# A planned order of instructions made anew (later weight loads, ten early T buffers, three raw weight buffers), and the last output tile stored in two halves

## The chip, the cores and the metric

One NeuronCore of a Trainium2 chip runs the whole program. The metric is the device time of one execution in microseconds; lower is better. Three runs of the kernel before gave a median of 514.42 us (514.08 to 516.64).

## What is computed

Two stages follow each other. The first is a linear recurrence over 768 tokens for 4 batches of 8 heads of 48 dimensions; the second is a gated two-layer network on its 3,072 rows:

```python
# first stage, per batch and head
for t in range(S):                                   # S = 768
    cur = einsum('bhd,bhe->bhde', u * k[t], v[t])
    y[t] = einsum('bhd,bhde->bhe', r[t], state + cur)
    state = w * state + einsum('bhd,bhe->bhde', k[t], v[t])
# second stage, x = y as 3072 rows of 384
h = x @ w_in                                         # 384 x 2048
out = (h * cos(h)) @ w_out                           # 2048 x 384
```

The weights `w_in` and `w_out` arrive as 64-bit floats and are turned on the chip into a high and a low 32-bit part.

## The kernel before

**First stage.** The tokens are cut into 24 chunks of 128 tokens of one batch (`chunk`), in the order of time over all four batches. A chunk loads r, k and v (on the SP queue), multiplies r by k (POOL, L864), decays k (POOL, L874) and multiplies by u (POOL, L917), transposes k and r on TensorE (L833), forms a 128x128 product per head (L958), masks it (DVE, L963), multiplies by the state (L978) and by v (L989) into x, and makes the new state (L1004, DVE L1026 and L1027). x is split into a high and a low part (ACT L1179, DVE L1184). The first 12 chunks (`EARLY`) are done so, before and beside the start of the second stage; the other 12 are done later in halves of 64 tokens (`in_halves`, L1060 to L1123), between the matmuls of the second stage.

**Second stage.** Eight blocks of three chunks (384 tokens) go through 16 tiles of the hidden dimension, f = 0 to 15: 128 steps. A step has nine w_in matmuls (`mm_h`, L302), then a chain on ACT and DVE (L314, L317, L320, L1287, L1290, L1293), then nine w_out matmuls (`mm_o`, L309) into three PSUM accumulators. The first four blocks go through f = 0, 1, then through 2 to 4, then 5 to 9, then 10 to 15, and add their partial outputs in DRAM (`UNITS`, `CUTS`). So the first eight steps want only the tiles f = 0 and 1 of either weight.

**Weights.** `conv` turns one tile of raw weights into its two parts: a load on SP (w_in: six DMAs, L540; w_out: one, L561) into a buffer of the ring `R_raw`, ACT (L646), DVE (L654, L666), POOL (L677), ACT for the high part (L687), DVE for the low part (L694). There are 32 such tiles. `R_raw` has two buffers, and a third (`raw_r`) which is the memory of two of the four early r buffers (`r_all`) and comes free when the early chunks have used r. The ring `R_T`, from which a chunk takes four buffers, has eight.

**The order.** Every operation is an `Op` with an engine, a due date, a cost, a latency and the buffers that it takes. `Plan.order` makes the order of all engines before the program is built: `one_pass` picks, for each engine, among the operations that can start first the one with the earliest due date, and `latest` turns the result into new due dates for the next pass. The due dates of the first pass come from the program's formulas and from two tables of numbers, `CHUNK_DUE` and `TILE_SHIFT`. What comes out is one fixed order per engine; each engine, the SP queue too, works through its own list in that order and waits where an operand isn't there. Where the plan has TensorE idle before the first w_in matmul, `warm_up` puts matmuls on a zeroed tile (L1351), one for each 0.2 us of the planned gap.

**The end.** The last step's three w_out tiles of 384 columns are copied out of PSUM (ACT L1320, DVE L1322) and stored; the last one goes out on the ACT queue (L1331).

## Time and profile before

| what | value |
|---|---|
| median of 3 runs | 514.42 us (514.08 to 516.64) |
| profiled execution | 514.43 us, its span 512.7 us |
| TensorE busy | 498.7 us (97% of the span), 5,836 matmuls |
| DVE, ACT, POOL busy | 383.6, 314.0, 177.3 us |
| mean granted TensorE clock | 0.995 |
| data moved | 61.81 MB, 121 GB/s on the mean |

The span runs from the first instruction of the program to the last; the profiled execution's own time has 1.7 us around it. Times in the rows below are from the start of the span. A busy TensorE counts the warm-up matmuls too, so the first 60 us have to be read in the timeline. "Loads" are named here in units of 192 KB: r, k or v of one chunk is one unit, a raw weight tile of 384 KB two, and u one.

### The profile page before, as it was taken

The page shows a single profiled execution, that of the slowest core. Times are in us where ns is not written, and L with a number is a line of the kernel's source. Part 1 is how long each engine was busy: PE and PEld are TensorE (multiplying, and loading weights), DVE is VectorE, ACT ScalarE, POOL GpSimd, SP SyncE. Part 2 cuts the span into 40 slices and gives each one's busy share as a digit, 9 for nine tenths or more (in the row PEclk, how much of TensorE's full clock was granted, in tenths as well). Part 3 has the DMA queues.
Part 4 walks back from the last instruction along what each step waited for, and adds up shares of the span by engine and source line. Part 5 has one row for each costly group of instructions (what it writes and reads, how often), then busy time and mean ns, then how long its engine had stood idle before and what let it go on. Part 6 is the DMA issues. An engine that isn't in the chain of part 4 may idle for free.

```text
span 512.7 us, 14821 instructions
## 1 busy us (share of the span) xinstructions
PE 498.7 (97%) x5836; PEld 472.2 (92%) x5836; DVE 383.6 (75%) x788; ACT 314.0 (61%) x805; POOL 177.3 (35%) x183
## 2 busy tenths in 40 slices
PE   7999899999999999999999999999999999999994
PEld 5777789999999999999999999999999999999994
DVE  6888778889899996566777786767767777756452
ACT  1887676777776676547375665574663746654442
POOL 5876512246544463214426224133044042200000
PEclk9999899999999999999999999999999999999999
DMA  9978526577855875426484837448364475110001
GB/s 139 157 152 153 135 79 181 161 161 147 163 138 126 188 144 92 90 40 114 115 173 124 181 93 181 100 130 200 90 169 118 120 178 149 35 49 1 1 1 53
DMA packets 116657, 61.81 MB, mean 121 GB/s; under 512 B 80097, under 2 KB 112482, under 8 KB 116578
## 3 DMA queue, kind: packets, MB, share of 16 engines
q1 hardware_dynamic: 111250, 53.50, 43.0%
q0 software_dynamic: 5184, 7.08, 9.9%
q8 instruction: 47, 0.77, 0.7%
q14 instruction: 32, 0.26, 0.2%
q10 hardware_dynamic: 144, 0.20, 0.1%
HBM read 48.96 MB, written 11.80 MB: 118 GB/s over the span
## 4 chain that ended last, share of the span: by engine, by line
PE 88%; ACT 0%; issue 0%
PE psum L309 40%; PE psum L302 40%; PE psum L1123 4%; PE psum L1060 1%; PE psum L1076 1%; PE psum L989 1%; PE psum L958 0%; PE psum L978 0%; PE psum L1004 0%; PE psum L833 0%; ACT f L1320 0%; PE psum L605 0%
## 5 line engine op out<-in xcount | busy, mean ns | idle before, releaser
L309 PE MATMUL psum<-w_out_hi,gh 128*128 128x384 f32 x384 | 131.9, 344 | 0.0
L302 PE MATMUL psum<-xh,w_in_hi 128*128 128x384 f32 x384 | 131.5, 342 | 0.0
L309 PE MATMUL psum<-w_out_hi,gl 128*128 128x384 f32 x384 | 129.7, 338 | 0.0
L302 PE MATMUL psum<-xh,w_in_lo 128*128 128x384 f32 x384 | 129.7, 338 | 0.0
L309 PE MATMUL psum<-w_out_lo,gh 128*128 128x384 f32 x384 | 129.5, 337 | 0.0
L302 PE MATMUL psum<-xl,w_in_hi 128*128 128x384 f32 x384 | 129.4, 337 | 0.0
L314 ACT ACTIVATE qi<-psum 128x384 int32<-128x384 f32 (+1 forms) x132 | 62.9, 479 | 79.6 <-PE psum L302 78.8
L317 DVE SCALAR_TENSOR_TENSOR f<-psum,qi 128x384 f32<-128x384 f32 (+1 forms) x132 | 71.0, 540 | 47.4 <-ACT qi L314 46.6
L1293 DVE TENSOR_TENSOR gl<-f,gh 128x384 fp32r<-128x384 f32 (+1 forms) x132 | 83.9, 639 | 28.9 <-ACT gh L1290 28.0
L1290 ACT CAST gh<-f 128x384 fp32r<-128x384 f32 (+1 forms) x132 | 65.8, 501 | 40.0 <-DVE f L1287 20.0
L320 ACT ACTIVATE f<-f 128x384 f32<-128x384 f32 (+1 forms) x132 | 67.6, 514 | 30.9 <-DVE f L317 30.4
L1287 DVE TENSOR_TENSOR f<-psum,f 128x384 f32<-128x384 f32 (+1 forms) x132 | 70.6, 537 | 12.8 <-ACT f L320 10.9
L309 PEld LDWEIGHTS psum<-w_out_hi,gh 128*128 128x128 f32 x384 | 72.0, 187 | 2.4 <-issue 0.2
L302 PEld LDWEIGHTS psum<-xh,w_in_hi 128*128 128x128 f32 x384 | 72.5, 189 | 1.6 <-ACT T L942 0.2
L302 PEld LDWEIGHTS psum<-xl,w_in_hi 128*128 128x128 f32 x384 | 72.6, 189 | 0.0
L302 PEld LDWEIGHTS psum<-xh,w_in_lo 128*128 128x128 f32 x384 | 72.6, 189 | 0.0
L309 PEld LDWEIGHTS psum<-w_out_hi,gl 128*128 128x128 f32 x384 | 72.0, 188 | 0.0
L309 PEld LDWEIGHTS psum<-w_out_lo,gh 128*128 128x128 f32 x384 | 72.0, 187 | 0.0
L852 POOL TENSOR_TENSOR T<-T,decT_k 112x512 f32<-112x512 f32 x12 | 17.0, 1414 | 126.7 <-DVE T L847 50.8
L1335 POOL DMA_DIRECT2D out_dram<-f x36 | 33.3, 1080 | 41.0 <-ACT f L1320 40.6
L677 POOL TENSOR_TENSOR f<-f,raw 128x384 int32<-128x384 int32 x23 | 26.2, 1138 | 48.0 <-ACT gh L1290 15.7
L942 ACT ACTIVATE T<-ident,a 128x128 f32<-128x128 f32 x96 | 30.2, 391 | 1.2 <-DVE a L923 1.2
(124 smaller groups left out, 610.8 us busy)
## 6 DMA issues: line engine op xcount, KB each, us to landing
raw<-in_moe_w_out_dram SPq DMA_DIRECT2D x23, 384.0 KB, 3.6
out_dram<-f POOLq DMA_DIRECT2D x36, 192.0 KB, 5.0
raw<-in_moe_w_in_dram SPq DMA_DIRECT2D x72, 64.0 KB, 2.4
out_dram<-f SPq DMA_DIRECT2D x23, 192.0 KB, 2.0
r_all<-in_r_dram SPq DMA_DIRECT2D x40, 96.0 KB, 2.3
raw<-in_moe_w_in_dram SPq DMA_DIRECT2D x10, 384.0 KB, 4.0
raw<-in_k_dram SPq DMA_DIRECT2D x39, 96.0 KB, 2.2
v<-in_v_dram SPq DMA_DIRECT2D x18, 192.0 KB, 4.4
```

Of the source, the lines that this page charges most:

```text
L302: nc.tensor.matmul(ph, a, b_, start=(i == 0), stop=(i == len(mm) - 1))
L309: nc.tensor.matmul(acc, a[:, ts], b_, start=(first and i == 0), stop=(last and i == 2))
L314: nc.scalar.activation(qi, ph, AF.Copy, scale=INV_2PI, bias=0.25)
L317: nc.vector.scalar_tensor_tensor(q, ph, INV_2PI, qi, op0=ALU.mult, op1=ALU.subtract)
L320: nc.scalar.activation(q, q, AF.Sin, scale=TWO_PI, bias=0.5 * math.pi)
L677: lambda: nc.gpsimd.tensor_tensor(ai(), ai(), cn(), op=ALU.add),
L942: nc.scalar.activation(A[j]()[:, p, :], ident, AF.Copy, scale=ab()[:, h : h + 1])
L1123: nc.tensor.matmul(xv()[G * g : G * g + G, kk, tokens(n)], lhsT, rhs, start=(kk // 2, g) not in opened, stop=True, skip_group_check=True,)
L1287: nc.vector.tensor_tensor(g()[:, cs], ph()[:, cs], q()[:, cs], op=ALU.mult)
L1290: nc.scalar.copy(gh()[:, cs], g()[:, cs])
L1293: nc.vector.tensor_tensor(gl()[:, cs], g()[:, cs], f32(gh())[:, cs], op=ALU.subtract)
L1335: nc.gpsimd.dma_start(dst, ob(), accum_op=ALU.add)
```

## The change

The tables `CHUNK_SHIFT` (24 entries, added to due dates from one formula) and `TILE_SHIFT` (32 entries) replace the two old ones, and there are seven passes for six. In the plan, an operation that issues DMAs gets a time for which its data move (`dma`), the moves are taken one after another, and an issue counts as startable at the earliest 3 us before the moves ahead of it end; costs of some operations are others. The r buffers of the early chunks are four of their own (before: two of their own and two in `r_all`), so `R_raw` has three buffers of its own from the start. Early chunks take T buffers from ten. The parts of w_out kept from the start are 8 tiles for 10. Warm-ups may stand up to the first w_out matmul. The last w_out tile is computed, copied and stored as two halves of 192 columns, the first through DVE and the SP queue, the second through ACT and its queue. The matmuls and other operations are the same but for that tile and the warm-ups (78 for 65).

```diff
-CHUNK_DUE = (-17.2, -100.0, -17.0, -16.6, -14.0, -12.8, -11.2, -10.1, -1.3, 1.2, 13.7, 37.7)
-TILE_SHIFT = (-9.7, 1.9, -82.4, -2.9, -12.4, 2.4, -14.7, 11.2, 1.4, 0.6, 6.8, 16.5)
-PASSES = 6
+CHUNK_SHIFT = (
+    -11.6, -28.5, -0.3, -1.6, 3.2, -4.4, 2.1, -0.2, -0.1, -1.5, 1.6, 0.7, -6.4, -53.9, -19.5, 1.4,
...
+PASSES = 7
+DMA_AHEAD, DMA_FIRST, DMA_LAST, DMA_LAND = 3.0, 1.3, 0.6, 1.95
...
-                        feas.append((max(free[eng], r[0], port if o.port else 0.0), o, r[1]))
+                        t = max(free[eng], r[0], port if o.port else 0.0, moved - DMA_AHEAD if o.dma else 0.0)
+                        feas.append((t, o, r[1]))
...
+            if o.dma:
+                moved = max(moved, t + DMA_FIRST) + o.dma
+                o.lat = max(moved + DMA_LAST - o.end, DMA_LAND)
...
-    F_1 = CUTS[-2]
+    F_1 = NF // 2
...
-        r_all = att.tile([P, 2, H, DP], F32, name="r_all")
-        R_r = [Tile(r_all[:, i]) for i in range(2)]
-        raw_r = Tile(r_all.rearrange("q i h d -> q (i h d)")[:, 0 : 2 * DM].bitcast(I32).rearrange("q (f w) -> q f w", w=2))
...
-        X_r = early_ring("r", 2, [P, H, DP])
+        X_r, X_T = early_ring("r", 4, [P, H, DP]), early_ring("T", 2, [P, NP, C])
...
-        R_raw = ring("raw", 2, [P, DM, 2], I32) + [raw_r]
+        R_raw = ring("raw", 3, [P, DM, 2], I32)
...
-                rb, kb, vb = Buf(R_r + X_r), Buf(R_k + X_k), Buf(R_v + X_v)
+                rb, kb, vb = Buf(X_r), Buf(R_k + X_k), Buf(R_v + X_v)
...
-            kT, rT = Buf(R_T), Buf(R_T)
+            R_Tc = R_T + X_T if i < EARLY else R_T
+            kT, rT = Buf(R_Tc), Buf(R_Tc)
...
-                due = CHUNK_DUE[i]
+                due = -1.5 * (EARLY - i) - 1.0
...
+            due += CHUNK_SHIFT[i]
...
-            if i < len(TILE_SHIFT):
-                due += TILE_SHIFT[i]
+            due += TILE_SHIFT[i]
...
+                jc = FIRST[n] + t
+                last = jc == NJ - 1 and f == f1 - 1
+                ends = [slice(0, DM // 2), slice(DM // 2, DM)] if last else [slice(0, DM)]
+                for e, cs in enumerate(ends):
...
+                        mm_o(acc(), gh(), gl(), f, t, f == f0, f == f1 - 1 and cs.stop == DM, cs)
...
+                    eng = DVE if t % 2 or (last and e == 0) else ACT
...
+                    q = ACT if last and eng == ACT else POOL if f0 and not last else SP
```

How the order moves, at three places. On the SP queue, the loads of the last early chunks (k and r in pairs of DMAs of four heads each, v in one) and of the first weights; before:

```order
L540 DMA raw1_128<-in_moe_w_in_dram 32x2x256 x4
L540 DMA raw1_128<-in_moe_w_in_dram 64x256 x2
L763 DMA early_k1_90<-in_k_dram 128x4x48 x2
L763 DMA early_r0_95<-in_r_dram 128x4x48 x2
L755 DMA v2_83<-in_v_dram 128x8x48
L763 DMA early_k2_91<-in_k_dram 128x4x48 x2
L763 DMA early_r1_96<-in_r_dram 128x4x48 x2
L755 DMA early_v0_92<-in_v_dram 128x8x48
L561 DMA raw0_127<-in_moe_w_out_dram 128x768
```

and now:

```order
L551 DMA raw0_130<-in_moe_w_in_dram 32x2x256 x4
L551 DMA raw0_130<-in_moe_w_in_dram 64x256 x2
L782 DMA early_r2_96<-in_r_dram 128x4x48 x2
L782 DMA early_k1_89<-in_k_dram 128x4x48 x2
L774 DMA v2_82<-in_v_dram 128x8x48
L551 DMA raw1_131<-in_moe_w_in_dram 32x2x256 x4
L551 DMA raw1_131<-in_moe_w_in_dram 64x256 x2
L782 DMA early_r3_97<-in_r_dram 128x4x48 x2
L782 DMA early_k2_90<-in_k_dram 128x4x48 x2
L774 DMA early_v0_91<-in_v_dram 128x8x48
L774 DMA early_v1_92<-in_v_dram 128x8x48
L572 DMA raw2_132<-in_moe_w_out_dram 128x768
```

The first w_in tile (raw0) stood behind 21 units of r, k and v and now stands behind 28. The second (raw1) stood before k and r of the eleventh chunk and now stands behind them and its v. In front of the last load of the twelfth chunk there were 38 units (u, twelve k, twelve r, nine v, two raw tiles of two each, its own counted), and there are 38 now.

On POOL, the products of the last early chunk, `f<-early_r,early_k`, and the sums that end the conversion of a raw tile, `f<-f,raw`; before:

```order
L864 TENSOR_TENSOR f7_120<-early_r1_96,early_k2_91 128x384
L677 TENSOR_TENSOR f4_117<-f4_117,raw1_128 128x384
L874 TENSOR_TENSOR early_k2_91<-early_k2_91,dec_k_133 128x2x4x48
L917 TENSOR_TENSOR f7_120<-f7_120,u_b_129 128x384
L677 TENSOR_TENSOR f8_121<-f8_121,raw0_127 128x384
```

and now:

```order
L883 TENSOR_TENSOR f5_121<-early_r3_97,early_k2_90 128x384
L696 TENSOR_TENSOR f4_120<-f4_120,raw0_130 128x384
L893 TENSOR_TENSOR early_k2_90<-early_k2_90,dec_k_137 128x2x4x48
L936 TENSOR_TENSOR f5_121<-f5_121,u_b_133 128x384
L696 TENSOR_TENSOR f7_123<-f7_123,raw1_131 128x384
```

The sum behind the twelfth chunk's first product was that of the second w_in tile; it is now that of the first, and the second's comes three operations later.

On ACT now, from the high part of the first w_in tile to that of the second (`raw2` holds w_out for f = 0, and `raw0` by then w_out for f = 1, loaded a second time):

```order
L706 CAST w_in_hi_66<-f4_120 128x3x128
L961 ACTIVATE early_T0_98<-ident_64,a1_84 128x128 x4
L961 ACTIVATE T2_102<-ident_64,a1_84 128x128 x2
L1198 CAST xh_114<-psum_76 128x384
L961 ACTIVATE T2_102<-ident_64,a1_84 128x128 x2
L665 ACTIVATE raw2_132<-raw2_132 128x384
L665 ACTIVATE raw0_130<-raw0_130 128x384
L326 ACTIVATE qi0_125<-psum_76 128x384
L706 CAST w_in_hi_66<-f7_123 128x3x128
```

Before, the two casts of w_in stood 19 rows apart with only the second tile's own L646 between them; now the first passes over two w_out tiles stand ahead of the second cast.

On TensorE the list up to the second step's w_in matmuls holds the same work but for one chunk's products with state and v (L978 and L989 before, L997 and L1008 now): ahead of them stand 12 chunks' transposes, 11 chunks' L958, 9 of L1004 and the first step's nine w_in matmuls in either program, with 5 and 9 chunks of L978 and L989 before, and 6 and 10 now. The first step's matmuls stood behind the ninth chunk's transposes; they now stand directly ahead of the twelfth's.

## Rows read from the trace of the kernel before

**Rows 1.** The page's busy time of TensorE (part 1: busy us, share of the span, instructions) and the granted clock in 40 slices of the span (part 2, tenths of full speed).

```profile
PE 498.7 (97%) x5836; PEld 472.2 (92%) x5836; DVE 383.6 (75%) x788; ACT 314.0 (61%) x805; POOL 177.3 (35%) x183
...
PEclk9999899999999999999999999999999999999999
```

**Rows 2.** The page's part 4, the chain of waits that ended last: shares of the span by engine.

```profile
PE 88%; ACT 0%; issue 0%
```

**Rows 3.** Busy time by stretch. Columns: the stretch in us, its length, then for PE, PEld, DVE, ACT and POOL the busy us and the instructions in it, the granted TensorE clock, the DMA engines' share and what they moved.

```profile
10.00:20.00 10.00, 8.02 (x142) 6.66 (x144) 9.04 (x18) 6.37 (x20) 8.37 (x9) 1.00 1.33 155
20.00:30.00 10.00, 9.92 (x241) 8.17 (x237) 8.36 (x17) 9.58 (x29) 8.89 (x10) 1.00 0.89 162
30.00:40.00 10.00, 9.22 (x268) 7.19 (x270) 9.15 (x19) 8.64 (x26) 5.96 (x7) 1.00 0.71 141
40.00:50.00 10.00, 9.02 (x225) 7.37 (x213) 7.78 (x17) 6.69 (x20) 6.37 (x7) 1.00 0.78 158
50.00:60.00 10.00, 7.98 (x152) 6.90 (x135) 8.36 (x18) 7.18 (x22) 6.72 (x6) 0.86 0.87 186
...
100.00:150.00 50.00, 50.00 (x288) 50.00 (x287) 46.45 (x89) 35.99 (x82) 25.17 (x25) 1.00 0.68 152
```

**Rows 4.** The same view with finer stretches.

```profile
58.00:60.00 2.00, 2.00 (x8) 2.00 (x7) 1.84 (x4) 1.62 (x6) 0.00 (x0) 0.50 0.46 137
```

**Rows 5.** The chain of waits in order of time, merged: start us, us, what.

```profile
93.17 1.56 PE psum L302 x9
```

**Rows 6.** Timeline of TensorE. Columns: start us, us from the first start to the last end, line, operation, tiles, how many; in brackets the idle time before and what ended it.

```profile
49.56 0.67 PE L978 MATMUL psum<-T,s 48*32 48x128 f32 x32
50.16 1.08 PE L989 MATMUL psum<-T,v 128*32 128x128 f32 x32
51.17 0.56 PE L1004 MATMUL psum<-v,k 128*48 128x48 f32 x16
...
53.43 1.16 PE L958 MATMUL psum<-T,T 48*128 48x128 f32 x16
56.14 0.44 PE L833 MATMUL psum<-ident,early_k 64*112 64x64 f32 x8 [1.55 <-POOL early_k L874]
...
56.64 1.42 PE L958 MATMUL psum<-T,T 48*128 48x128 f32 x16
57.98 0.69 PE L302 MATMUL psum<-xh,w_in_hi 128*128 128x384 f32 x1
...
60.71 0.34 PE L302 MATMUL psum<-xh,w_in_lo 128*128 128x384 f32 x1
```

**Rows 7.** Timeline of POOL, same columns.

```profile
48.63 1.02 POOL L864 TENSOR_TENSOR f<-early_r,early_k 128x384 f32<-128x384 f32 x1 [3.47 <-DMA early_r<-in_r_dram]
...
53.13 1.01 POOL L864 TENSOR_TENSOR f<-early_r,early_k 128x384 f32<-128x384 f32 x1 [0.65 <-DVE a L923]
54.10 1.02 POOL L677 TENSOR_TENSOR f<-f,raw 128x384 int32<-128x384 int32 x1
55.07 1.01 POOL L874 TENSOR_TENSOR early_k<-early_k,dec_k 128x384 f32<-128x384 f32 x1
```

**Rows 8.** Timeline of the SP queue (SPq: the time in which SP issues the loads of a row, its waits included).

```profile
39.91 3.42 SPq L540 DMA_DIRECT2D raw<-in_moe_w_in_dram  x6
43.45 1.63 SPq L763 DMA_DIRECT2D early_k<-in_k_dram  x2
...
48.02 1.01 SPq L763 DMA_DIRECT2D early_r<-in_r_dram  x2
...
49.67 1.86 SPq L561 DMA_DIRECT2D raw<-in_moe_w_out_dram  x1
```

**Rows 9.** DMA issues from 0 to 84 us: tiles, queue, how many, KB each, median us from issue to landing.

```profile
early_r<-in_r_dram SPq DMA_DIRECT2D x12, 96.0 KB, 4.1
...
raw<-in_moe_w_out_dram SPq DMA_DIRECT2D x3, 384.0 KB, 3.2
```

**Rows 10.** What the SP queue waited for from 0 to 70 us: line, releaser, us in total, times, longest.

```profile
SPq L763 <- PE psum L989: 1.2, 1, 1.2
SPq L763 <- POOL f L864: 0.7, 2, 0.4
SPq L763 <- PE psum L302: 0.7, 1, 0.7
```

**Rows 11.** Timeline of DVE, two steps of the conversion of the second w_in tile.

```profile
50.10 0.54 DVE L666 SCALAR_TENSOR_TENSOR f<-raw,f 128x384 int32<-128x384 int32 x1
...
55.69 0.81 DVE L694 TENSOR_TENSOR w_in_lo<-f,w_in_hi 128x384 fp32r<-128x384 f32 x1 [0.23 <-ACT w_in_hi L687]
```

**Rows 12.** Timeline of ACT, the step between them.

```profile
55.15 0.51 ACT L687 CAST w_in_hi<-f 128x384 fp32r<-128x384 f32 x1 [1.52 <-POOL f L677]
```

**Rows 13.** Timeline of the end of the run.

```profile
505.64 0.34 PE L309 MATMUL psum<-w_out_lo,gh 128*128 128x384 f32 x1
506.02 0.48 ACT L1320 COPY f<-psum 128x384 f32<-128x384 f32 x1 [0.58 <-PE psum L309]
506.53 0.38 ACTq L1331 DMA_DIRECT2D out_dram<-f  x1
```

**Rows 14.** DMA issues from 505 us to the end.

```profile
out_dram<-f ACTq DMA_DIRECT2D x1, 192.0 KB, 3.4
```

**Rows 15.** Timeline of TensorE at the start, the four transposes of the decay table.

```profile
11.57 0.66 PE L501 MATMUL psum<-ident,decT_k 128*128 128x128 f32 x4 [1.79 <-DVE decT_k L485]
```

More of the change, by code (lines that the diff above doesn't have):

```diff
@@ L86, in __init__, with op @@
         self.lines = {}
-    def op(self, eng, due, cost, emit, after=(), bufs=(), lat=0.2, line=None, port=False):
-        o = Op(eng, due, cost, lat, emit, after, bufs, self.lines.get(line) if line else None, port)
+    def op(self, eng, due, cost, emit, after=(), bufs=(), lat=0.2, line=None, port=False, dma=0.0, behind=None):
+        o = Op(eng, due, cost, lat, emit, after, bufs, self.lines.get(line) if line else behind, port, dma)
         if line:
@@ L191, in one_pass @@
                 cand.setdefault(o.eng, []).append(o)
-        done, port = [], 0.0
+        done, port, moved = [], 0.0, 0.0
         while len(done) < len(self.ops):
@@ L308, in mm_o @@
         for i, (a, b_) in enumerate(mm):
-            nc.tensor.matmul(acc, a[:, ts], b_, start=(first and i == 0), stop=(last and i == 2))
+            nc.tensor.matmul(acc[:, cs], a[:, ts], b_[:, cs], start=(first and i == 0), stop=(last and i == 2))
     def whole(qi, ph):
@@ L639, in cn @@
                 return raw()[:, :, 0]
-            o0 = op(SP, due - 3.5, 1.6 if part else 3.2, lambda: load_raw(i, raw, True), [behind], [raw], lat=3.4)
+            o0 = op(
+                SP,
+                due - 3.5,
+                0.5 if part else 4.2,
+                lambda: load_raw(i, raw, True),
+                [behind],
+                [raw],
+                dma=1.4 if part else 1.5,
+            )
             o2 = op(
@@ L782, in chunk @@
                 ks, rs = Buf(R_raw), Buf(R_raw)
[L784 removed]
+            rbs = [rb]
             def load_r():
@@ L934, in early @@
             def early():
-                A = [Buf(R_T) for _ in range(2)]
+                A = [Buf(R_Tc) for _ in range(2)]
                 Ap = [Buf(B_ONE) for _ in range(2)]
@@ L1313 @@
                     ob = Buf(R_f)
-                    jc = FIRST[n] + t
                     row = (jc % B) * S + (jc // B) * C
-                    dst = out[row : row + C, :]
-                    def cp(acc=acc[t], ob=ob, t=t):
-                        if t % 2 == 0:
-                            nc.scalar.copy(ob(), acc()[:, 0:DM])
-                        else:
-                            nc.vector.tensor_copy(ob(), acc()[:, 0:DM])
-                    oc = op(ACT if t % 2 == 0 else DVE, s + 2.3, 0.45, cp, [oo], [acc[t], ob])
@@ L1327, with cp @@
-                    last = jc == NJ - 1
-                    def st(ob=ob, dst=dst, f0=f0, last=last):
-                        if last:
-                            nc.scalar.dma_start(dst, ob())
-                        elif f0 == 0:
-                            nc.sync.dma_start(dst, ob())
+                    dst = out[row : row + C, cs]
+                    eng = DVE if t % 2 or (last and e == 0) else ACT
+                    def cp(acc=acc[t], ob=ob, eng=eng, cs=cs):
+                        if eng == ACT:
+                            nc.scalar.copy(ob()[:, cs], acc()[:, cs])
+                        else:
+                            nc.vector.tensor_copy(ob()[:, cs], acc()[:, cs])
```

88 lines of the change are left out of this document (56 added, 32 removed).

## The prediction

> **What bounds the kernel now.** I read the page first, then the chain of waits, then busy time by stretch, and only then the timelines of the first 60 us. TensorE is busy 97% of the span at a clock that is full but for one stretch [rows 1], and 88% of the chain that ended last is TensorE [rows 2]. From 100 to 150 us it is busy in every microsecond [rows 3], so nothing that DVE, ACT or POOL gain there can shorten the run; a change of order there can only harm. What can be won lies ahead of the steady part: in the five stretches from 10 to 60 us TensorE is busy 44.2 us of 50, and part of that is warm-ups [rows 3]. A nine-matmul step at full speed takes 1.56 us [rows 5]. The second step starts at 57.98 us, after an idle 1.55 us in which TensorE waited for POOL's decayed k of the twelfth chunk [rows 6].
>
> I therefore measure the change at one point: when the second step's w_in matmuls start, and how much work stands behind them. From there on I hold TensorE to be the limit, as it is now.
>
> What leads to that point is the arrival of the twelfth chunk's k and r. I call it L. Before, SP issued the last r pair at 48.02 us over 1.01 us, so the second half at about 48.5 [rows 8]; such a load lands 4.1 us later [rows 9]: L = 52.6. POOL's product starts at 53.13, a weight sum follows, then the decay at 55.07, and the transposes start at 56.14 [rows 6, 7]. Ahead of this POOL had stood idle 3.47 us for the eleventh chunk's r [rows 7], which SP could issue only after 3.42 us spent on the six DMAs of the second w_in tile [rows 8].
>
> **The loads.** The change moves raw tiles behind chunk loads, but 38 units stand ahead of the end of the twelfth chunk's loads in either order, so L gains only what waits disappear. SP's r and k loads show 2.6 us of waits up to 70 us [rows 10]; with all of them gone L would be 50.0, with none 52.6. The stretches from 20 to 50 us moved 162, 141 and 158 GB/s; at 162 throughout, the last 20 us would shrink by 20 x (1 - 299 / 324) = 1.5 us, which lies between. The early r buffers are four before and after, so they free nothing. Two more T buffers let a chunk's product start sooner, but no row that I rest on waits for a T buffer. I take the middle: half of the waits gone, **L = 51.3**.
>
> **From L to the second step.** Now the first w_in tile's sum stands behind the twelfth chunk's first product on POOL. So the first step, which ran at 42 us before, must now wait for L as well: product 0.97 us (53.13 to 54.10), sum 0.97 (54.10 to 55.07) [rows 7], ACT's cast 0.51 [rows 12], DVE's low part 0.81 [rows 11], together L + 3.3. Its nine matmuls take 1.56 [rows 5]; the twelfth chunk's transposes 0.50 (56.14 to 56.64), then another chunk's products with state 0.60 (49.56 to 50.16) and with v 1.01 (50.16 to 51.17) [rows 6]: L + 6.9. The second w_in tile runs beside it: three more POOL operations at 0.97 bring its sum to L + 4.9. But ACT has two w_out passes ahead of its cast, and the second of them reads a buffer that POOL frees at L + 1.9, into which 384 KB are loaded in 3.2 us [rows 9]: L + 5.1. Three ACT operations at about 0.51 [rows 12] and DVE's 0.81 [rows 11] then give L + 7.5. I take L + 7.2, so the second step starts at 58.5, 0.5 us later than the 57.98 of before. In exchange one chunk's L978 and L989, 0.60 + 1.01 = 1.6 us, then stand behind it that did not before. Net: **1.1 us won**; 2.4 at L = 50.0, 0.2 lost at L = 52.6.
>
> **The clock.** From 58 to 60 us the granted clock is 0.50, that is 1.2 GHz of 2.4 [rows 4], after the stretch in which TensorE waited for the twelfth chunk. The eight matmul starts from 57.98 to 60.71 took 2.73 us [rows 6] where eight ninths of 1.56 [rows 5] are 1.39: 1.3 us lost. The fall may come again or stay away, so the gain lies between 0 and 1.3. The wait for the first step's weights is an idle stretch of the same kind, but TensorE has one chunk's products more to do before it. I take half, **0.6 us won**. The Trainium skill, in "TensorE: Matmul & The Clock Gate" (What's actually happening), says that "the default state is throttled, and activity releases the throttle". By that a TensorE that waits for the weights falls again, this term is nothing and the sum is 513.2; the row at 58 us bears the rule out for an idle stretch of this length.
>
> **The end.** The last w_out tile now takes six matmuls of 192 columns for three of 384. Nine of 384 pace at 1.56, so three are about 0.52. At half the columns six cost the same 0.52; at the pace of the four 128-column transposes (0.66 for four [rows 15]) they would cost 0.99, which is 0.47 more. I take 0.1 more, nearer to the column count. The Trainium skill's "TensorE: Matmul & The Clock Gate" (LDWEIGHTS) gives a weight load as its columns over 1.2 in ns, an estimate of 0.107 us for 128; six would then be 0.64, which is 0.1 more and speaks against this part of the change. The transposes' row is in line with it. The last copy, 0.48 us for 384 columns [rows 13], falls to between 0.24 and 0.48, say 0.35; the last store, issued at 506.53 and landing 3.4 us later [rows 13, 14], has half the bytes, which can win from nothing to half of 3.4, and I take 0.1, since two other stores are still under way and the same bytes move. Together **0.1 us won**, from 0.5 lost to 1.9 won.
>
> **Parts that cost nothing.** The start up to the second chunk's transposes keeps its chain (the decay table at 11.57 [rows 15], idle 1.79 on DVE) and its warm-ups, 47 for 48. The 13 further warm-ups fill planned gaps; where a gap isn't there in fact they cost at most 13 x 0.17 = 2.2 us, by the row of the four transposes, and this belongs to the slower case's bound. The split of w_out into 8 and 8 tiles and the store on SP are covered by a TensorE that is always busy from 100 us; without that cover, a late w_out tile would cost its conversion, 0.54 + 1.02 + 0.51 + 0.81 = 2.9 us [rows 7, 11, 12]. The late loads are unchanged in number and lie in the same cover.
>
> **Sum.** 1.1 + 0.6 + 0.1 = 1.8 us. The profiled execution took 514.43 us (span 512.7), the median of the runs is 514.42, so no correction: **512.6 us**. A measurement of this kernel tells about 0.5% (2.6 us) from no change.
>
> **Rivals.**
> (B) The loads flow: SP's waits go altogether, L = 50.0, and TensorE does not slow. For it: the DMA engines' share fell from 1.33 to 0.71 and 0.78 between 30 and 50 us [rows 3], so there was room; the new plan spaces the loads. Against it: the same bytes, and SP's issue times remain. Second step at 57.2, 0.8 + 1.6, clock 1.3, end 0.1: 3.8 won, 510.6 us (509.2 to 511.7).
> (E) The order brings the loads no earlier: L = 52.6, second step at 59.8, 0.2 lost, the clock falls as before: 514.5 us. For it: the last chunk has as many units ahead as ever, so the change would not do what its late loads say.
> (C) Slower: ACT stands at the w_out pass for f = 1 while the second w_in tile waits behind it. If its load takes not 3.2 but 5.6 us, because the eleventh and twelfth chunks' v and another w_out tile lie ahead of it, and L stays 52.6, the second step starts at 62.2 instead of 59.8, 2.6 us lost net, and the clock's 1.3 once more: 518.3 us, 515.5 to 519. It decides from a landing later than about L + 6. For it: all w_out loads now come in one bunch behind the chunks. Against it: SP need not wait for a buffer there any more (1.86 us at 49.67 [rows 8]).
> (D) A stall in the steady part. DVE is busy 46.45 of 50 us there [rows 3], and the order converts some w_out tiles a step nearer to their use. Two tiles late by 2.9 us each, less the 1.8: 518.4 us. Against it: not one wait of TensorE in that stretch today.
>
> **How the numbers follow.** Forecast 0.38 (511.0 to 513.9), B 0.33, E 0.14, C 0.11, D 0.04. Faster than 511.85 are nearly all of B and a quarter of the forecast: 0.42. Slower than 517.0 by the same bound: most of C and D, 0.14 with E's upper edge. Between them 0.44. The range leaves out most of C, D and the lowest of B: 509.2 to 516.0; the forecast's own is 511.0 to 513.9.
>
> **What would show it.** Right: the first step's w_in matmuls near 54.6, behind a POOL sum that waited for the twelfth chunk's r; the second step at about 58.5 with six chunks of L997 done; no wait of TensorE after it; the last copy near 0.35. Wrong: a first step before 50 us (then the first tile did not wait for L), a second step before 57 or after 60, a wait of TensorE on w_out between 100 and 450 us, or a clock at 0.50 for longer than before.

## The result, and the profile after

The changed kernel takes **517.55 us** (median of 8 runs, 516.29 to 520.19) against 514.52 for the kernel before beside it (8 runs): ratio 1.0065, 95% interval 1.0040 to 1.0091. It was forecast 512.6, in 509.2 to 516.0, so it is slower and lies outside the range. The profiled execution took 517.61 us, its span 515.9 against 512.7: 3.2 us to account for.

The page of the profile after, which answers to [rows 1] (busy time of TensorE, and the granted clock in 40 slices):

```profile
PE 501.7 (97%) x5852; PEld 473.4 (92%) x5852; DVE 382.3 (74%) x789; ACT 315.8 (61%) x805; POOL 173.9 (34%) x183
...
PEclk9997999999999999999999999999999999999998
```

TensorE is busy 3.0 us longer with the same work but for 13 warm-ups and the halved tile, and the slice with the low clock is the fourth (39 to 52 us), no longer the fifth. From 60 us to the end no wait of TensorE is listed, as before. So the time goes ahead of 60 us or behind the last matmul. Busy time by stretch, after, as in [rows 3, 4] (columns: length, then busy us and instructions of PE, PEld, DVE, ACT, POOL, then granted clock, DMA share, GB/s):

```profile
40.00:42.00 2.00, 1.34 (x28) 1.10 (x22) 1.01 (x2) 0.66 (x2) 1.92 (x3) 1.00 0.23 60
42.00:44.00 2.00, 1.15 (x23) 0.99 (x25) 1.87 (x5) 1.83 (x6) 1.95 (x2) 1.00 0.65 142
44.00:46.00 2.00, 2.00 (x25) 1.55 (x23) 1.57 (x3) 2.00 (x7) 0.00 (x0) 0.66 0.74 135
46.00:48.00 2.00, 2.00 (x37) 1.55 (x43) 1.63 (x4) 1.20 (x4) 1.54 (x2) 0.50 0.79 197
48.00:50.00 2.00, 2.00 (x52) 1.49 (x40) 1.67 (x4) 0.00 (x0) 1.45 (x2) 0.50 0.23 66
50.00:52.00 2.00, 2.00 (x64) 1.23 (x60) 0.28 (x1) 1.22 (x4) 0.00 (x0) 0.64 0.85 158
```

"Busy 2.00" hides the loss here: at a clock of 0.66, 0.50, 0.50 and 0.64 these 8 us do the work of 4.6, 3.4 lost. The like rows of before lose 1.7, from 56 to 62 us (0.82, 0.50, 0.82; the middle one is [rows 4]):

```profile
56.00:58.00 2.00, 1.86 (x33) 1.64 (x33) 1.76 (x3) 2.00 (x8) 1.37 (x2) 0.82 0.75 228
60.00:62.00 2.00, 2.00 (x11) 2.00 (x11) 0.78 (x2) 0.92 (x3) 0.00 (x0) 0.82 0.11 33
```

And after, in 48 to 50, ScalarE does nothing at all. Why, its timeline tells, with those of VectorE and GpSimd (start, length, what; in brackets the idle time ahead of it and who ended it):

```profile
46.65 0.55 ACT L665 ACTIVATE raw<-raw 128x384 int32<-128x384 uint32 x1
50.78 0.56 ACT L665 ACTIVATE raw<-raw 128x384 int32<-128x384 uint32 x1 [3.58 <-DMA raw<-in_moe_w_in_dram]
51.23 0.46 ACT L1198 CAST xh<-psum 128x384 fp32r<-128x384 f32 x1
...
56.02 0.51 ACT L706 CAST w_in_hi<-f 128x384 fp32r<-128x384 f32 x1
```

```profile
51.72 0.56 DVE L1203 TENSOR_TENSOR xl<-psum,xh 128x384 fp32r<-128x384 f32 x1 [2.06 <-ACT xh L1198]
...
58.01 0.54 DVE L713 TENSOR_TENSOR w_in_lo<-f,w_in_hi 128x384 fp32r<-128x384 f32 x1
```

```profile
53.36 1.01 POOL L883 TENSOR_TENSOR f<-early_r,early_k 128x384 f32<-128x384 f32 x1 [3.91 <-DVE a L942]
54.32 1.02 POOL L696 TENSOR_TENSOR f<-f,raw 128x384 int32<-128x384 int32 x1
```

ScalarE stands 3.58 us at the raw w_in columns for f=1, with a cast of xh behind them that VectorE waits for. GpSimd stands at the twelfth chunk's product, with the weight sum for f=0 behind it. Its 3.91 us are put down to VectorE, which was long done; the chain names the transfer, `50.55 2.65 DMA early_k<-in_k_dram`. TensorE's timeline, as in [rows 6]:

```profile
42.85 0.44 PE L852 MATMUL psum<-ident,k 64*112 64x64 f32 x8 [1.51 <-POOL f L883]
...
54.57 0.44 PE L852 MATMUL psum<-ident,early_k 64*112 64x64 f32 x8 [0.27 <-POOL f L883]
...
58.81 0.56 PE L1023 MATMUL psum<-v,k 128*48 128x48 f32 x16
59.30 0.45 PE L314 MATMUL psum<-xh,w_in_hi 128*128 128x384 f32 x1
...
61.07 0.44 PE L852 MATMUL psum<-ident,early_k 64*112 64x64 f32 x8
...
63.27 0.45 PE L314 MATMUL psum<-xh,w_in_hi 128*128 128x384 f32 x1
```

The first step starts at 59.30 (before 42.25), the second at 63.27 (before 57.98). From 54.57 on no wait of TensorE is listed: it comes to the first step at 59.30 straight from its work ahead of it, and the step's weights were ready 0.75 us sooner (VectorE's low part, 58.01 + 0.54). The SP queue, as in [rows 8]:

```profile
44.63 4.08 SPq L551 DMA_DIRECT2D raw<-in_moe_w_in_dram  x6
48.82 1.08 SPq L782 DMA_DIRECT2D early_r<-in_r_dram  x2
50.00 1.00 SPq L782 DMA_DIRECT2D early_k<-in_k_dram  x2
```

The twelfth chunk's loads end on SP at 51.00 and land at 53.2. Their issues still stand behind the six transfers for f=1. The end, as in [rows 13]:

```profile
507.61 0.27 PE L321 MATMUL psum<-w_out_lo,gh 128*128 128x192 f32 x1
508.30 1.70 SPq L1368 DMA_DIRECT2D out_dram<-f  x1
508.31 0.32 ACT L1356 COPY f<-psum 128x192 f32<-128x192 f32 x1 [1.09 <-DVE f L1358]
508.66 0.38 ACTq L1366 DMA_DIRECT2D out_dram<-f  x1
```

(The third row's idle time is put down to VectorE's copy of the first half.) The last matmul starts at 507.61, 1.97 us later than the 505.64 of before, and the span ends 8.31 us behind it instead of 7.10. **So 2.0 us are lost ahead of the last matmul and 1.2 behind it.** [rows 14] had the last store, 192 KB on ScalarE's queue, land 3.4 us after its issue; now SP's half lands 3.9 us after its own and is the last to land:

```profile
out_dram<-f SPq DMA_DIRECT2D x1, 96.0 KB, 3.9
out_dram<-f ACTq DMA_DIRECT2D x1, 96.0 KB, 3.0
```

Counted from the start of the last matmul, that is 4.6 us (508.30 + 3.9 - 507.61) against 4.3 before (506.53 + 3.4 - 505.64). So only 0.3 of the 1.2 us is a later landing; the other 0.9 lies between the last landing and the end of the span.

### The profile page after: what moved, and what is told of

Read it like the earlier page. It is cut to its first block, busy times and chain, and to the rows that moved or that the text cites. A ratio compares the mean times of both kernels' runs of the same rounds, so it can differ in the third digit from the quotient of the medians.

```text
span 515.9 us, 14842 instructions
## 1 busy us (share of the span) xinstructions
PE 501.7 (97%) x5852; PEld 473.4 (92%) x5852; DVE 382.3 (74%) x789; ACT 315.8 (61%) x805; POOL 173.9 (34%) x183
## 4 chain that ended last, share of the span: by engine, by line
PE 92%; SPq 3%; DMA 1%; POOL 1%; issue 1%; DVE 0%; ACT 0%; POOLq 0%; ACTq 0%
PE psum L321 40%; PE psum L314 39%; PE psum L1142 3%; SPq L782 2%; PE psum L977 2%; PE psum L1008 2%; PE psum L1079 1%; PE psum L997 1%; DMA early_r<-in_r_dram 1%; PE psum L852 1%; PE psum L1095 1%; PE psum L1023 1%; POOL f L883 1%; PE psum L1386 1%; DMA early_k<-in_k_dram 1%
## 5 line engine op out<-in xcount | busy, mean ns | idle before, releaser
L314 PE MATMUL psum<-xh,w_in_hi 128*128 128x384 f32 x384 | 129.9, 338 | 0.0
L696 POOL TENSOR_TENSOR f<-f,raw 128x384 int32<-128x384 int32 x32 | 37.0, 1179 | 67.0 <-DVE f L685 26.1
L866 DVE STREAM_TRANSPOSE T<-raw 128x512 f32<-128x512 f32 x24 | 26.4, 1113 | 0.0
```

Of the source, the lines that this page charges most:

```text
L314: nc.tensor.matmul(ph, a, b_, start=(i == 0), stop=(i == len(mm) - 1))
L696: lambda: nc.gpsimd.tensor_tensor(ai(), ai(), cn(), op=ALU.add),
L866: nc.vector.transpose(dst().rearrange("q p (t g) -> q p g t", g=4), blocks)
```

## Experiments

Two profiles of one order of work differ by up to 1.9 us at the last matmul (507.61 after, 509.49 in the first run below), so a profile tells where an engine stands, and times are compared by their medians. "Against before" is the ratio to runs of the kernel before on the same chip, with its 95% interval.

**The last tile whole** (`tail_whole`).

```diff
-                ends = [slice(0, DM // 2), slice(DM // 2, DM)] if last else [slice(0, DM)]
+                ends = [slice(0, DM)]
-                    eng = DVE if t % 2 or (last and e == 0) else ACT
+                    eng = DVE if t % 2 else ACT
```

Expected: 

> The changed kernel with the last output tile undivided (one copy of 384 columns, one store), everything else in the same order. In the changed kernel the last w_out matmul ends at 507.90 and the span at 515.9, 8.0 us later; before it was 506.00 and 512.7, 6.7 us. Theory A (the loss has two parts, and the halves are one of them: the second copy waits for the first, 0.4 us, and SP takes 1.70 us to issue the first half's store, so that the end is put off): last matmul still at 507.9 (+-0.3), end 6.7 us behind it, span 514.6, 1.3 us won. Rival B (all of the 3.2 us are lost ahead of the last matmul and the end of the span varies by itself): span 515.9 +-0.3.

Measured: 517.35 us, 1.0032 (0.9999 to 1.0065). Last matmul at 509.49, the end 7.18 us behind it. The end is shorter by the 1.1 us that theory A wants; its span isn't, since this execution lost 1.9 us more ahead of the last matmul. The order ahead of the tail looks slower by itself: 2.2 us in the medians, with an interval that just reaches 1. The changed kernel itself took 517.55, 0.2 us more, so what the halves cost doesn't show in the times.

**Halves alone** (`tail_only`): the kernel before, its last tile emitted in the same halves.

Expected: 

> The kernel before with nothing changed but its last output tile, in two halves of 192 columns: VectorE copies the first and SP stores it, ScalarE copies and stores the second. Theory A: last matmul at 506.0, end 8.0 us behind it instead of 6.7, span 514.0, 1.3 us slower than before. Rival B: span 512.7 +-0.3. The forecast on record would have it 0.1 us faster than before (0.5 slower to 1.9 faster).

Measured: 515.74 us against 515.12, 1.0006 (0.9974 to 1.0038); 7.90 us from the last matmul to the end. The trace has the cost, 0.8 us; the times can't resolve it.

**Which part of the halves?** Both of these kernels were executed once; their cuts of the diff are against `tail_only`. `tail_one_store`: copies in halves, one store by ScalarE.

```diff
-                            nc.sync.dma_start(dst[:, HALVES[0]], ob()[:, HALVES[0]])
-                            nc.scalar.dma_start(dst[:, HALVES[1]], ob()[:, HALVES[1]])
+                            nc.scalar.dma_start(dst, ob())
```

Expected: 

> The kernel before with the last tile multiplied and copied in two halves, but stored whole by ScalarE once both copies are done. From the start of the last matmul to the end of the span it took 7.10 us before and 7.90 with two stores. If the copies one behind the other are the cost: 7.5 to 7.9. If the extra store is the cost: 7.1 to 7.3 (the last store begins some 0.2 us later than before).

`tail_two_sp`: two stores for the halves, and the first of the last three tiles stored by ScalarE, so that SP issues two.

```diff
+                        elif ahead2:
+                            nc.scalar.dma_start(dst, ob())
-                        ACT if last else SP if f0 == 0 else POOL,
+                        ACT if last or ahead2 else SP if f0 == 0 else POOL,
```

Expected: 

> The kernel before with the last tile in two halves with two stores, and the first of the last three tiles stored by ScalarE instead of SP, so that SP's queue issues two stores and not three (its third issue took 1.70 and 1.27 us, against 0.34 for the two ahead of it). If SP's queue is the cost: that issue back at some 0.35 us and 7.0 to 7.3 from the last matmul's start to the end. If any store of half rows on SP is slow to issue or lands late: 7.7 to 8.3 again.

Measured from the last matmul to the end: 6.61 us with one store, 8.08 with two. The SP issue of the half:

```profile
504.83 0.35 SPq L1345 DMA_DIRECT2D out_dram<-f  x1
505.28 0.83 SPq L1340 DMA_DIRECT2D out_dram<-f  x1
```

Halves stored in two parts end in 8.31, 8.08 and 7.90 us (three profiles, mean 8.1). Whole stores end in 6.5 to 7.4 in thirteen profiles of this study and in 8.24 in a fourteenth (mean 7.1). Copied in halves and stored whole, it is 6.61. So two stores cost about 1.0 us, and the 192-column matmuls and copies don't; with one execution of that kind and such a spread this is likely rather than settled. It costs even where SP issues only two. The cost isn't a later arrival: with two stores the last one lands 4.6, 4.0 and 3.9 us behind the start of the last matmul, whole ones at 3.8 to 4.6. From the last landing to the end of the span it is 3.7, 3.9 and 4.1 us with two stores, and 2.3 to 3.6 with whole ones. What that time goes into stays open, and so does what makes SP slow to issue the half (1.70, 1.27, 0.83 us; ScalarE's half takes 0.34 to 0.38). The slow issue alone isn't enough: in `plan_only`, below, SP took 1.68 us for a whole store, and the end came 7.0 us behind the last matmul's start.

**Buffers or tables?** `bufs_only` puts the new buffers into the kernel before; `plan_only` puts the old buffers into the changed kernel with a whole last tile.

Expected: 

> The kernel before with the new buffers alone (four early r tiles of their own, two early T tiles more, three raw tiles, eight w_out tiles in the first pool): due dates, costs and the planner as before, last tile whole. The planner may lay out another order, since it counts the buffers. Theory C (the tables and the planner's account of the loads lose the 1.9 us ahead of the last matmul, not the buffers): within 1 us of before, last matmul 505 to 507. Rival D (the buffers do it: the early T tiles and w_out tiles take room, or the ring of r now hands tiles out in an order that makes SP wait): last matmul at 507.5 or later.

Expected: 

> The changed kernel with the buffers of before (r in two shared and two early tiles, no early T, raw in two tiles and the shared one, ten w_out tiles first) and the last tile whole: only the tables, the costs and the planner's account of the loads are new. Theory C: last matmul at 507.5 or later, since the order is what costs, and worse than the changed kernel, as the tables were fitted to other buffers (508 to 512). Rival D: last matmul at 505 to 507, as before.

Measured: buffers alone 515.64 against 515.12, 0.9997 (0.9963 to 1.0032), last matmul at 507.45, in between the two theories; tables alone 523.14, 1.0140 (1.0077 to 1.0203), last matmul at 512.73. The buffers by themselves cost nothing that can be measured. The tables fit only the buffers that they were made for, so this run doesn't price them. That the loss goes with the new order follows by elimination here; the runs below move parts of that order.

**Which wait in the new order?** From here on a few operations are moved by hand in the order that the planner gives, in the kernel with a whole last tile (517.35 us). `act_free` moves ScalarE's conversion for f=1 back, `loads_first` the loads for f=1 behind the twelfth chunk's, `both` does both (577 and 576 are their numbers in the plan):

```diff
+        behind(seq[577], seq[166])   # act_free, both: L665 for f=1 behind two xh casts
+        behind(seq[576], seq[256])   # loads_first, both: raw w_in for f=1 behind the twelfth r and k
```

Expected: 

> The changed kernel with the last tile whole, and one instruction moved: ScalarE's conversion of the raw w_in columns for f=1 (L665) stands behind the two xh casts that followed it, so that ScalarE doesn't wait for that load (3.58 us from 47.2 to 50.78 in the changed kernel, with the xh casts, VectorE's xl and then TensorE behind it). Theory H1 (this wait is what loses the time between 47 and 60, as TensorE's idle and then its half clock): xh at 49.5 to 50 instead of 51.2, no stretch of half clock after it, second step at 60 to 61.5 instead of 63.3 to 65.3, last matmul 505.5 to 507, span 512.5 to 514 (514.4 to 517 without it). Rival H2 (the landing of the twelfth chunk's k and r, 53.3 to 54.3, sets the step): second step and span within 0.7 us of the kernel without the move.

Expected: 

> The changed kernel with the last tile whole, and one load moved on SP: the six transfers of the raw w_in columns for f=1 (44.6 to 48.7) go behind the twelfth chunk's r and k instead of ahead of them. Those land some 4 us sooner (about 49 to 50 instead of 53.3 to 54.3), the raw columns some 2.2 us later (about 52.5 to 53 instead of 50.4 to 50.8), and ScalarE still stands at them. H1: 1.5 to 2.5 us slower than without the move, second step at 65 or later. H2: 2 to 4 us faster, second step at 59.5 to 61.5.

Expected: 

> Both moves together, last tile whole: the twelfth chunk's r and k ahead of the raw columns for f=1, and ScalarE's conversion of those behind the two xh casts. H1: as the conversion moved alone or 0 to 1 us better. H2: as the loads moved alone, 2 to 4 us faster than neither. If both waits count, one behind the other, this is the fastest of the three, span 511 to 513.

Measured: 517.92 (1.0062, 1.0039 to 1.0086), 520.70 (1.0120, 1.0094 to 1.0146) and 518.30 us (1.0060, 1.0036 to 1.0084). Neither theory gets its gain. Later raw columns do harm as H1 said, but freeing ScalarE alone wins nothing. In `act_free` GpSimd's order takes over. Its rows of GpSimd, ScalarE and TensorE:

```profile
53.73 1.02 POOL L883 TENSOR_TENSOR f<-early_r,early_k 128x384 f32<-128x384 f32 x1 [4.57 <-DMA early_k<-in_k_dram]
54.70 1.02 POOL L696 TENSOR_TENSOR f<-f,raw 128x384 int32<-128x384 int32 x1
```

```profile
55.76 0.51 ACT L706 CAST w_in_hi<-f 128x384 fp32r<-128x384 f32 x1 [2.13 <-POOL f L696]
...
57.94 0.46 ACT L1198 CAST xh<-psum 128x384 fp32r<-128x384 f32 x1
```

```profile
58.45 0.88 PE L1023 MATMUL psum<-v,k 128*48 128x48 f32 x16 [2.05 <-ACT xh L1198]
```

The sum for f=0 waits behind the product that waits for the twelfth k; ScalarE stands at that sum, with xh behind it; TensorE waits 2.05 us, and its clock is 0.59 and 0.56 from 58 to 62. In `both` the load is early, but ScalarE stands at f=1 all the same, one place further on, now with a copy of kT behind it:

```profile
53.81 0.55 ACT L665 ACTIVATE raw<-raw 128x384 int32<-128x384 uint32 x1 [3.06 <-DMA raw<-in_moe_w_in_dram]
54.26 0.57 ACT L931 COPY T<-psum 112x512 f32<-112x512 f32 x1
```

```profile
54.92 0.44 PE L852 MATMUL psum<-ident,early_k 64*112 64x64 f32 x8 [2.92 <-POOL f L936]
```

So both theories fall, and theory S takes their place: several engines have ready work queued behind work that waits for a load, and each such place hides the next. It was put to four runs, on one chip: `f0_ahead`, `both_late`, `decay_first` (a place of the same kind at 18 to 22 us) and `all_moves`:

```diff
+        ahead(seq[566], seq[259])    # f0_ahead, all_moves: sum for f=0 ahead of the twelfth product
+        behind(seq[577], seq[166])   # f0_ahead: as in act_free
+        behind(seq[577], seq[247])   # both_late, all_moves: further back
+        behind(seq[576], seq[256])   # both_late, all_moves: as in loads_first
+        ahead(seq[84], seq[127])     # decay_first, all_moves: fourth decay ahead of the sixth product
```

Expected: 

> Last tile whole; ScalarE's conversion of the raw columns for f=1 behind the two xh casts as in the run where it alone was moved, and also GpSimd's weight sum for f=0 (L696) ahead of the twelfth chunk's product, which waits for its loads until 53.7. In the run with the one move ScalarE then stood 2.13 us at that sum, the next xh came 2 us late, TensorE waited 2.05 us at 58.45 and its clock fell behind that. Theory S: with the sum at 50.4 that wait goes and so does the half clock: second step 61 to 62.5 instead of 64.36, 2 to 3.5 us faster than the one move alone. Rival L (it is the landing of the twelfth chunk's k, 53.7, that sets the second step, not the order behind it): second step 63.5 to 65 again, within 0.7 us.

Expected: 

> Last tile whole; the twelfth chunk's r and k are loaded ahead of the raw columns for f=1, and ScalarE's conversion of those comes only behind the tenth chunk's diagonals (with the conversion behind the two xh casts ScalarE still stood 3.06 us there, with the copy of the eleventh chunk's kT behind it, and TensorE waited 2.92 us). Theory S: ScalarE no longer stands, transposes of the eleventh chunk at 52 instead of 54.92, no half clock after, second step 60 to 62 instead of 65.12, 3 to 4.5 us faster. Rival L: as the landing is already early in that run, nothing more comes: within 0.7 us of it.

Expected: 

> The changed kernel with the last tile whole, and one GpSimd instruction moved: the decay of the fourth chunk's k (L893) ahead of the product of the sixth chunk (L883), which waits for that chunk's r (1.61 us from 18.2 to 19.77 in the changed kernel); TensorE's transposes of the fourth chunk wait for that decay and ran at 21.79. Theory S (the order puts work that is ready behind work that waits for a load, in several places one after the other, each hiding the next): those transposes at 19.3 to 20.2, 1 to 2 us less lost between 20 and 24, but the later places (ScalarE at the raw columns for f=1, GpSimd at the twelfth product) stay, so the second step comes 0 to 1.5 us sooner than 63.3 to 65.3 and the time is within 1.5 us of the kernel without the move. Rival E (the time lost at 20 to 24 is simply carried to the end): 1.5 to 2.5 us faster.

Expected: 

> Last tile whole; all four moves: the fourth chunk's decay ahead of the sixth's product, the twelfth's r and k ahead of the raw columns for f=1, ScalarE's conversion of those behind the tenth chunk's diagonals, GpSimd's sum for f=0 ahead of the twelfth's product. Theory S: second step 58 to 60.5, span 511 to 513, as fast as the kernel before or up to 2 us faster. If the buffers and the length of the work, not waits at loads, set the time, it stays over 514.5.

| run | median us | against before | second step | clock under 1.0 |
|---|---|---|---|---|
| `f0_ahead` | 515.05 | 1.0011 (0.9987 to 1.0036) | 61.69 | none from 38 to 66 us |
| `both_late` | 516.45 | 1.0029 (1.0004 to 1.0054) | 61.74 | none |
| `decay_first` | 517.15 | 1.0046 (1.0018 to 1.0075) | 65.36 | 52 to 60 us |
| `all_moves` | 515.57 | 1.0017 (0.9992 to 1.0041) | 60.82 | none |

`f0_ahead` is 2.9 us faster than `act_free` (0.5% by the ratios, as the two ran on different chips), with one more instruction moved, and is no longer to be told from before. On its own chip it is 2.1 us faster in the medians than `decay_first`, whose move won nothing (2.7 +- 1.3 in the means of 12 runs each). The landing of the twelfth k can't be the reason, for in this run it is as late as ever:

```profile
49.95 1.02 POOL L696 TENSOR_TENSOR f<-f,raw 128x384 int32<-128x384 int32 x1 [0.55 <-ACT xh L1198]
53.99 1.02 POOL L883 TENSOR_TENSOR f<-early_r,early_k 128x384 f32<-128x384 f32 x1 [3.02 <-DMA early_k<-in_k_dram]
```

The sum's move alone, without that of `act_free`, wasn't run. And the next place of the kind shows at once: VectorE stands at the raw w_out columns with xl behind them, ScalarE at its own w_out passes (3.0 us from 44 to 64) with the cast for f=1 behind them, and TensorE waits 1.32 us for xl:

```profile
58.06 0.36 DVE L673 TENSOR_SCALAR f<-raw 128x384 int32<-128x384 int32 x1 [2.21 <-DMA raw<-in_moe_w_out_dram]
59.49 0.56 ACT L665 ACTIVATE raw<-raw 128x384 int32<-128x384 uint32 x1 [0.86 <-DMA raw<-in_moe_w_out_dram]
60.08 0.67 PE L997 MATMUL psum<-T,s 48*32 48x128 f32 x32 [1.32 <-DVE xl L1203]
```

In `both_late` and `all_moves` ScalarE stands there for 2.6 and 2.2 us. `both_late` won 1.9 us over `both` in the medians, less than the 3 to 4.5 expected, and the two intervals overlap. `decay_first` moved the fourth transposes from 21.79 only to 20.71, and nothing came of it at the end, as S said: time won where a later wait follows is waited away there (TensorE waits 2.2 us for xl ahead of 51.74 in this run, 1.6 ahead of 51.97 in `tail_whole`). `all_moves` wins no more than `f0_ahead`; its interval reaches 1, but its median is over 514.5, which by the expectation speaks for the buffers and the length of the work. By S it is the wait for w_out that is left in it; no run decides between the two.

**Wait or clock?** `act_free_warm` puts 16 warm-ups into the 2.05 us wait of `act_free`:

```diff
+                    if o.seq == 208:
+                        n = 16
```

Expected: 

> The run with ScalarE's conversion behind the two xh casts alone, with 16 warm-up matmuls put ahead of the state product (L1023) for which TensorE then waited 2.05 us (56.4 to 58.45), after which its granted clock was 0.59 and 0.56 in the next two stretches of 2 us. If the half clock behind the wait costs by itself what the rows say (0.41 and 0.44 of 2 us, 1.7 us): clock 1.0 there, second step at 62.5 to 63 instead of 64.36, 1.3 to 2 us faster than 517.9. If the clock falls anyway (later, or at the next wait): within 0.7 us.

Measured: 517.21 us, 1.0024 (0.9996 to 1.0052). The clock held, and in that profile the second step started at 62.93 instead of 64.36, 1.4 us sooner; its stretches:

```profile
58.00:60.00 2.00, 1.64 (x23) 1.47 (x23) 1.76 (x6) 1.46 (x5) 0.92 (x1) 1.00 0.33 121
60.00:62.00 2.00, 2.00 (x57) 1.49 (x59) 1.89 (x4) 1.72 (x4) 0.11 (x1) 1.00 0.39 88
```

The medians differ by 0.7 us, which these intervals don't resolve. By the two traces the slow clock behind a wait of 2.05 us cost up to 1.4 us more. That the warm-ups kept the clock up isn't shown by one profile each, for a wait without them isn't always followed by a slow stretch. In `tail_only`, with the order of before, TensorE waits at the same place as before and as long, and its clock stays at 1.00:

```profile
56.24 0.44 PE L833 MATMUL psum<-ident,early_k 64*112 64x64 f32 x8 [1.66 <-POOL early_k L874]
```

```profile
58.00:60.00 2.00, 2.00 (x13) 2.00 (x13) 1.82 (x4) 2.00 (x7) 0.00 (x0) 1.00 0.47 150
```

**The same place in the order of before** (`swap_before`, and once more as `swap_again`): there the twelfth k and r also stood behind the six transfers for f=1.

```diff
+        for o, x in ((581, 225), (583, 264), (580, 264), (579, 243), (577, 210), (578, 243), (576, 257)):
+            behind(seq[o], seq[x])
```

Expected: 

> The kernel before (its buffers, tables and tail) with the same moves made in its order: the raw w_in columns for f=1 are loaded behind the twelfth chunk's k and r, and the four steps of their conversion go behind what they would otherwise hold up (ScalarE: behind the tenth chunk's xh cast; VectorE: behind the eleventh chunk's reduction; GpSimd: behind the twelfth chunk's decay and u; the raw w_out columns for f=1 behind that). Before, those k and r landed at 52.6, the twelfth transposes ran at 56.14 and the second step began at 57.98. H2: landing about 49, transposes about 53, second step 55.5 to 56.5, span 510.5 to 512. H1 (that landing isn't what holds this order): second step within 0.7 us of 57.9, span as before.

Expected: 

> The kernel before with the raw columns for f=1 loaded and converted behind the twelfth chunk, run a second time since 513.33 against 514.75 was within the error. If the order of before also loses time at those columns: 1 to 2 us faster than before again, the interval of the ratio wholly below 1. If not: within 0.5 us of before.

Measured: 513.33 against 514.75 (0.9981, 0.9952 to 1.0010) and 513.93 against 515.23 (0.9980, 0.9949 to 1.0011). It is 1.3 to 1.4 us lower both times and has the lowest medians of the study, but each interval reaches past 1, so that it beats the kernel before isn't shown. The second step came at 57.70 and 58.48, not at 55.5 to 56.5: with the load early, the conversion for f=1 stands in the chain of waits that leads to the step.

## Why the prediction was wrong, step by step

- **What bounds.** Right: no wait of TensorE after 60 us, and the second step is the place to measure at. In all ten profiles of the new order with its own buffers the last matmul starts 444.2 to 444.6 us behind it. Rival D (a stall in the steady part) didn't come. In the terms of the sum: the second step is 5.3 us later, not 0.5; 3.3 us less stand behind it (444.3 against 447.7), of which 1.4 are the slow clock (in `tail_only`, with the order of before and no slow stretch, it is 446.3) and 1.9 the work, forecast as 1.6; the end loses 1.2. That makes the 3.2. Two of its own signs of being wrong came: a second step after 60 us, and a clock at 0.50 for longer than before.
- **The loads, L = 51.3.** Wrong by 1.9 us: L is 53.2, later than its upper bound of 52.6. Before, the last half of r, issued at 48.53, landed 4.4 us later, at 53.0, so the change hardly moved L. "Half of the waits gone" failed. From 14 us to the end of the twelfth loads SP's r and k loads waited 3.0 us by the listed waits before and 4.4 after; 2.2 of the 4.4 are for GpSimd's decays. I had said that the early r buffers free nothing, and they didn't; the waits stayed with the order.
- **From L to the second step, L + 7.2.** This is the step that failed most: it took L + 10.1 (63.27). I had seen that the sum for f=0 stands behind the twelfth product, and priced the chain behind it as if each engine were free, and as if TensorE stood ready when the weights came. Neither was so. The weights of the first step were there at 58.55, some L + 5.3 instead of L + 3.3: ScalarE's cast stood behind a copy of kT (55.55, from a transpose that itself ran late) and VectorE's low part behind e_r and two masks (58.01). TensorE came later still, at L + 6.1, without a wait since 54.57: it was behind with its own work, after a wait of 1.51 us (to 42.85) and the 3.4 us lost at a low clock from 44 to 52. In `tail_whole`, the second profile of this order, the weights are there at 59.0 and TensorE comes at 61.37. There the delay is ScalarE's stand at the raw columns for f=1: xh and VectorE's xl are late by it, TensorE waits for xl, and its clock is low behind that wait:

```profile
50.42 0.54 ACT L665 ACTIVATE raw<-raw 128x384 int32<-128x384 uint32 x1 [3.29 <-DMA raw<-in_moe_w_in_dram]
```

```profile
51.97 0.56 PE L1023 MATMUL psum<-v,k 128*48 128x48 f32 x16 [1.62 <-DVE xl L1203]
```

```profile
54.00:56.00 2.00, 2.00 (x26) 1.74 (x26) 1.19 (x4) 1.82 (x6) 1.70 (x2) 0.50 0.90 233
```

So what the prediction had wrong is the path: not L and one chain behind it set the step, but work queued behind work that waits for loads, from 41 us on. That such places cost, and not L by itself, `f0_ahead` shows: L as late as ever, two of them taken out, 2.1 us faster than `decay_first`. What each of them costs by itself in the changed order wasn't measured. The work gained ahead of the second step was there (one chunk's L997 and L1008).
- **The clock, 0.6 won.** Behind the second step, where the term was priced, it came out at its upper bound: no granted clock under 1.00 follows 63.27 until the last matmul, and the 1.3 to 1.4 us of before are saved. But a slow stretch came ahead of the step, 3.4 us of work lost where before lost 1.7 in all, behind a wait at 41.3 us that I didn't foresee; it is part of the L + 10.1. Half was a fair price for a thing that differs between executions of one order: `tail_only` has none behind 1.66 us of waiting. The Trainium skill's "TensorE: Matmul & The Clock Gate" (What's actually happening), which I set beside this term, has throttling as the default and activity as what lifts it. The rows from 44 to 52 us agree with it; but "the row at 58 us bears the rule out for an idle stretch of this length" went too far from one row, since `tail_only` kept 1.00 behind as long a wait.
- **The end, 0.1 won (0.5 lost to 1.9 won).** Wrong, outside its bounds: 1.2 us lost, some 1.0 by the mean of the profiles. The pace of the 192-column matmuls was about right (six take 0.65, by their spacing of 0.11 from 507.07 on). The 0.66 us for four transposes, which gave the upper bound of 0.99, has the length of the last one in it; their starts lie 0.11 apart too. The two copies run one after the other (0.36 and 0.32 us), so ScalarE's store is issued 1.05 us behind the last matmul's start and not 0.89. The second store, on SP, which I had counted as a small gain, is the last to land, 0.3 us later than the whole store of before; 0.9 come behind the last landing, where the prediction had no term, and their cause stays open. A rule bears on the copies that the prediction didn't use: the Trainium skill's "PSUM — Partial Sum Buffer" (PSUM bank collisions raise a hardware error) says that two engines may not touch the same bank within the same partition at the same time, reads included. The trace agrees in so far as ScalarE's half waits for VectorE's and starts at 508.31, when that ends (508.28); no run here has two engines read one bank at once.
- **The rivals.** C had the sign and nearly the size (518.3 at a chance of 0.11), and its kind of wait, ScalarE standing at raw weights with other work behind; but the load was that of w_in for f=1, and not the w_out pass behind it, so its number is near by luck. C's own place comes to light in `f0_ahead`, once the earlier ones are moved. A list of every place where an engine's next instruction waits for a load might have given C more weight than B, which took for granted that loads flow.

## What to carry to other kernels

Where an order is searched with modelled load times, go through each in-order engine and look at what ready work stands behind an instruction that waits for a load: it is there that a load landing later than planned is paid, by engines that never asked for it. Such places lie one behind the other, so mending one may show nothing; follow the next wait before giving the theory up. Look at the trace of the tail before splitting a kernel's last store: here the split won nothing that a run shows, and three profiles end some 1.0 us later with it.

## What was not expected of the hardware

- A wait of 1.51 us (41.34 to 42.85) was followed, from 44 us on, by some 8 us with granted clocks of 0.50 to 0.66, mostly the lower of the two levels (1.2 GHz), while TensorE was busy without a gap. A wait isn't always followed by this: 1.56 us at the same place in `both` (41.41 to 42.97) and 1.66 in `tail_only` (54.58 to 56.24) were not, with 1.00 in the rows behind them. With sixteen warm-ups in a wait of 2.05 us it stayed at 1.00.
- SP took 0.83 to 1.70 us to issue a store of 128 half rows right behind whole ones that took it 0.34, and ScalarE 0.38 for the other half; in the run with the old buffers and new tables a second whole store took SP 1.68 us as well.
- One and the same order of work reached its last matmul 1.9 us apart in two executions, and all runs of the kernel before but one lay between 512.3 and 519.5 us. The 10 or 12 runs of a kernel made here give intervals of some 0.3% to either side, so a change smaller than that isn't told from none.
